# Exponentials in 504-column steps over one ring, a written list of products and expert pieces, and more places for weights and tokens in the tail

## The chip, the cores and the metric

The kernel runs on one core of one Trainium2 chip. The metric is the device time of one execution in microseconds (us), less being better. TensorE is called PE here, its weight loads PEld, VectorE DVE, ScalarE ACT and GpSimd POOL; SP only issues transfers.

## The reference, cut to what matters

```python
# q, k, v: (8, 8, 1152, 64) float32
q_pool = q.reshape(B, H, S // 2, 2, D).mean(axis=3)        # 576 queries a head
scores = (1 / sqrt(D)) * matmul(q_pool, k.transpose(0, 1, 3, 2))
attn = softmax(scores)
x = matmul(attn, v).transpose(0, 2, 1, 3).reshape(8 * 576, 8 * 64)   # 4608 tokens x 512
# mixture of experts: each token has one of 8 experts
for e in range(8):
    mask = domain_id == e
    out[mask] = maximum(x[mask] @ w1[e], 0) @ w2[e]       # 512 -> 1024 -> 512
```

## The kernel before

**Attention.** The 64 heads are taken in 32 pairs. For a pair, PE turns the keys and pooled queries (`turn`, 30 small transposes into one of three score buffers `s`, copied out by DVE into `kq` and `qz`). The scores are computed transposed: nine chunks of 128 keys stand on the partitions, 576 queries along the columns, so a pair has 9 x 576 = 5184 score columns. They are cut into 12 steps of 432 columns (`W`), and a step holds both heads, 864 numbers on each partition. `score(t)` writes a step into a buffer `s` of two PSUM banks (the pool has three of them), and `expo(t)` takes it through one ACT instruction into a buffer `e` of four steps (a ring of four). The maximum isn't subtracted. `av` is one product unit: 5 matmuls of 65 columns that add one chunk of one head, weighted sum and row sum at once, into a bank `acc`; there are 576 units, and after the ninth of a head `evac` divides on DVE into `xb`. When a batch is ready, `put_x` writes it to the token table `x_tok` in DRAM.

**Experts.** Tokens are sorted by expert on DVE during the attention, 5 tiles of 128 tokens for each of 8 experts, 40 tiles. A tile is gathered from `x_tok` (`get_x`, an indirect DMA issued by POOL), turned so that features stand on the partitions, multiplied by `w1` (32 matmuls of 128 columns), clipped at zero, multiplied by `w2` (8 matmuls of 512 columns) and scattered to `out` (POOL). While the attention runs, such tiles are done in pieces: `up` (4 matmuls of 128 columns) and `down` (1 matmul of 512 columns), 16 pieces and one turn a tile.

**What sets the order.** The order in the program is the order in each engine's queue. The main loop goes over `t`, the 384 steps; two steps form a window: score, exponential, the turn where there is one, score, exponential. After them come the product units of a fixed table (`AVS`, three units a window) and then as many pieces as the class `Fill` allows from estimated costs (`C_S`, `C_AV`, `C_P`, a budget `STEP` of 771 ns a step, and `SPAN` for three windows of a pair). 13 tiles are done that way.

**The tail.** After the last exponential come the last 12 units (one bank `acc`, first head to its end, then the second), then the last `put_x`, then the other 27 tiles as runs of tiles of one expert: `stage1` for all tiles of the run, then `stage2` tile by tile. Run 0 is expert 5's first three tiles, whose tokens are already turned in `xf`. The next run's tiles are gathered, and turned by PE (`turn_tile`) between the tiles of `stage2`, or by a transposing DMA on SP (`flip_x`) in the last four runs. Six experts' weights have places; the other two are loaded in the tail into places that come free.

Of the kernel before, what the change touches and what calls it, by code (L numbers as in the profile page):

```python
# [9 lines left out]
P = 128  # L10
# [9 lines left out]
def kernel(  # L20
# [49 lines left out]
    ering = att.enter_context(tc.tile_pool(name="ering", bufs=4))  # L70
# [3 lines left out]
    spsum = att.enter_context(tc.tile_pool(name="spsum", bufs=3, space=bass.MemoryType.PSUM))  # L74
# [7 lines left out]
    qz = [perm.tile([P, Sp], F16, name=f"qz_{i}") for i in range(2)]  # L82
    qps = [perm.tile([P, NJ, 2, D], F16, name=f"qp_{i}") for i in range(2)]
    v16 = [perm.tile([P, NC, 2, DV], F16, name=f"v16_{i}") for i in range(NV)]
# [74 lines left out]
    pre = spsum.tile([P, 2, 512], FP32, name="s")  # L159
# [57 lines left out]
    sc = [perm.tile([P, E, PADC + NT], FP32, name=f"sc{i}") for i in range(2)]  # L217
# [321 lines left out]
    def prep_v(p):  # L539
        nc.vector.tensor_copy(  # L540
            v16[p % NV][:, :, :, 0:D].rearrange("p c h d -> p h c d"), loaded[p]["vs"][:, :, :, :]
        )
# [15 lines left out]
    def turn(p):  # L558
        kp, qp = kpt[p], qpt[p]
        new_kq(p)  # L560
        mt = spsum.tile([P, 2, 512], FP32, name="s")[:, :, :].bitcast(F16)
# [21 lines left out]
    st, et, acc, xb = {}, {}, {}, {}  # L583

    def score(t):
        p, s_ = divmod(t, SPP)
        s = spsum.tile([P, 2, 512], FP32, name="s")
        st[t] = s
        o, u = 0, W * s_
        while o < W:  # L590
            c, q0 = divmod(u + o, Sp)
            n = min(Sp - q0, W - o)
# [7 lines left out]
    def expo(t):  # L600
        p, s_ = divmod(t, SPP)
        if s_ % 4 == 0:
            et[p, s_ // 4] = ering.tile([P, 2, 4 * W], F16, name="e")
        e_ = et[p, s_ // 4]
        o = W * (s_ % 4)
        nc.scalar.activation(  # L606
            e_[:, :, o : o + W], st.pop(t)[:, :, 0:W], AF.Exp, bias=0.0, scale=0.0625
        )

    def av(p, h, c, pool):  # L610
        if c == 0:
            acc[p, h] = pool[0].tile([P, 512], FP32, name=pool[1])
        for i in range(NQ):
            o = (c % 3) * Sp + QO[i]
            nc.tensor.matmul(  # L615
                acc[p, h][:, i * (D + 1) : (i + 1) * (D + 1)],
                lhsT=et[p, c // 3][:, h, o : o + P], rhs=v16[p % NV][:, c, h, 0 : D + 1],
# [20 lines left out]
    ends, cut = (nc.sync, nc.gpsimd), []  # L638

    def put_x(b, i):  # L640
        for lo, hi in zip(CUT, CUT[1:]):
            i_, m = (0, lo) if lo < 64 else (1 + (lo - 64) // P, (lo - 64) % P)
            if i_ == i:
# [7 lines left out]
                cut.append((b, i))  # L651
# [8 lines left out]
    def get_x(pool, e, i):  # L660
        x_ = pool.tile([P, Dm], F16, name="xs")
        mark(x_[0:1, 0:1], True)
        nb = [ib // NQ for k_, ib in zip(KO[1:], IB) if (i + 1) * P <= k_] + [B]
        gather(x_[:, :], grow[:, e * NTC + i : e * NTC + i + 1], nb[0])
# [12 lines left out]
    def load_part(e, j):  # L677
# [6 lines left out]
    AVS = {9 + 2 * g: [(g // 3, c, ACC) for c in range(3 * (g % 3), 3 * (g % 3) + 3)] for g in range(6)}  # L684
    AVS_END = {
        8: [(0, c, ACC) for c in range(4)],
        10: [(0, c, ACC) for c in range(4, 6)],
        12: [(0, c, ACC) for c in range(6, NC)],
        13: [(1, c, ACC) for c in range(NC)],
    }  # L690
    HOLES = ((0, 6), (0, 7), (0, 8), (1, 0))
    STEP, C_MODE, C_S, C_T, C_AV, C_X, C_P, LAG = 771, 190, 183, 440, 147, 220, 217, 250
    SPAN = {2: 1420, 4: 1700, 6: 1260}
# [50 lines left out]
    class Fill:  # L744
        def __init__(self):
            self.blocks, self.cur, self.ready = [], None, 0

        def open(self):
            return self.cur is not None or (self.blocks and self.blocks[0][3])

        def piece(self):
            if self.cur is None:
                self.cur = list(self.blocks.pop(0))
            self.cur[0].pop(0)()
            if not self.cur[0]:
                self.ready = now[0] + self.cur[2]
                self.cur = None

        def able(self, t):
            b = self.blocks[0] if self.blocks else None  # L760
            return b and (b[3] or b[4].get("t", NST) < t < NST - 8 and t >= WSTEP[b[4]["xs"][0]][3] + 14)

        def turns(self, t):
            h0 = tiles[len(turned0)] if len(turned0) < len(tiles) else None
            if h0 and len(turned0) <= len(begun) and got.get(h0["xs"], NST) + 10 <= t < NST - 13:
                return h0
            return None

    fb = Fill()

    turned, turned0, begun, tiles = [], [], [], []
# [13 lines left out]
    def add_tile(e, i):  # L785
        h0 = {"xs": (e, i)}
        tiles.append(h0)
# [33 lines left out]

        for fn, lo, hi in ((up, 0, 4), (up, 4, NF), (down, 0, NF)):
            fb.blocks.append((
                [lambda f=f, fn=fn: fn(f) for f in range(lo, hi)], 222, 1, (fn, lo) != (up, 0), h0
            ))
# [5 lines left out]
    GET = [112, 118, 140, 168, 188, 208, 213, 230, 248, 266]  # L831
    want = [(e, i, at) for (e, i), at in zip(early, GET)]
    want += [(FILL, 0, 296), (0, 2, 304), (FILL, 1, 310), (FILL, 2, 316), (1, 2, 322), (2, 2, 328)]
# [514 lines left out]
```

## Time and profile before

| | |
|---|---|
| median of 3 runs | 430.19 us |
| lowest and highest | 429.98 and 434.39 us |
| the profiled execution, first to last instruction | 436.5 us |
| PE busy, ACT busy, DVE busy | 393.5, 337.4, 229.8 us |
| first exponential starts, last one starts | 7.7 us, 319.5 us |
| first matmul of the tail's run 0 | 323.1 us |

The profiled execution's span is the only time of it that is listed; it is 1.015 of the median of the runs. ACT's work is nearly all exponentials and ends with the attention; PE works from start to end, but its busy time counts a matmul from its start to a modelled end, so that a stretch of matmuls that wait for each other also looks busy. What is read from it are starts, and the gaps that carry a releaser's name.

### The profile page before, as it was taken

What the parts mean: (1) busy time and instruction counts of PE and PEld (TensorE: products, weight loads), DVE (VectorE), ACT (ScalarE), POOL (GpSimd) and SP (SyncE); (2) the same over time, 40 slices, a digit from 0 to 9 for tenths busy, and PEclk for the clock granted to TensorE, in tenths of its full rate; (3) what the DMA queues carried; (4) which work ended last, traced back from release to release, by engine and by line L of the source; (5) the groups of instructions that cost most, each with busy time, mean ns of one, the idle gap of its engine ahead of it and who ended that gap; (6) DMA issues with size and microseconds to landing.
All of it is one profiled execution on the core that took longest, in us unless ns stands there. A gap on an engine that the chain in (4) does not pass through costs nothing. (4 is left out here: it accounts for less than half of the span.)

```text
span 436.5 us, 14439 instructions
## 1 busy us (share of the span) xinstructions
PE 393.5 (90%) x6230; PEld 257.5 (59%) x6230; DVE 229.8 (53%) x628; ACT 337.4 (77%) x445; POOL 185.6 (43%) x304
## 2 busy tenths in 40 slices
PE   7888888888999999999999989989977899999993
PEld 4555555555676766766676666666753565555451
DVE  4588779874565565555656555555331235223221
ACT  5999999999999999999999989999941233323220
POOL 4542233405272742271442436443427586442413
PEclk9699999999999999999999999999998999999999
DMA  8999999994999999798884879975913589998202
GB/s 214 219 234 210 221 233 229 215 221 104 216 230 246 235 222 238 175 230 173 202 191 69 187 132 212 194 179 98 175 52 106 129 158 171 213 172 186 106 25 94
DMA packets 55757, 77.66 MB, mean 178 GB/s; under 512 B 15343, under 2 KB 44432, under 8 KB 55682
## 3 DMA queue, kind: packets, MB, share of 16 engines
q0 software_dynamic: 38384, 66.93, 75.5%
q1 hardware_dynamic: 17026, 9.58, 10.7%
q8 instruction: 50, 0.82, 0.8%
q14 instruction: 25, 0.20, 0.2%
q10 hardware_dynamic: 272, 0.13, 0.1%
HBM read 95.46 MB, written 15.21 MB: 254 GB/s over the span
## 5 line engine op out<-in xcount | busy, mean ns | idle before, releaser
L606 ACT ACTIVATE e<-s 128x864 f16<-128x864 f32 x384 | 306.0, 935 | 7.1 <-PE s L594 4.7
L594 PE MATMUL s<-qz,kq 64*128 64x432 f16 (+2 forms) x1152 | 120.6, 289 | 13.8 <-ACT e L606 10.6
L615 PE MATMUL acc<-v,e 128*128 128x65 f16 x2880 | 121.2, 194 | 9.4 <-DVE xb L630 5.5
L615 PEld LDWEIGHTS <-e 128*128 128x128 f16 x2880 | 104.1, 98 | 38.2 <-DVE xb L630 17.4
L515 POOL DMA_INDIRECT out_dram<-osb,gid x40 | 42.5, 1063 | 80.2 <-DVE osb L816 36.8
L655 POOL DMA_INDIRECT xs<-x_tok,grow x40 | 42.6, 1064 | 74.9 <-DVE xs L93 16.1
L594 PEld LDWEIGHTS <-kq 64*128 64x128 f16 x1152 | 48.2, 94 | 42.8 <-issue 25.1
L114 POOL DMA_DIRECT2D vs<-in_v_dram x32 | 23.7, 741 | 61.0 <-DVE v L540 28.0
L1093 PE MATMUL op<-w2h,hT 128*128 128x512 f16 x208 | 48.3, 387 | 0.0
L1048 PE MATMUL hp<-xt,w1h 128*128 128x256 f16 (+3 forms) x320 | 43.4, 294 | 2.6 <-ACT hT L1053 2.1
L1048 PEld LDWEIGHTS <-w1h 128*128 128x128 f16 x352 | 31.8, 98 | 20.5 <-issue 3.2
L570 DVE COPY kq<-s 128x1152 f16<-128x1152 f16 x31 | 23.5, 758 | 36.1 <-PE s L565 33.7
L1055 DVE TENSOR_SCALAR hT<-hp 128x256 f16<-128x256 f32 (+2 forms) x36 | 20.1, 558 | 40.8 <-PE hp L1048 32.1
L1099 ACT COPY osb<-op 128x512 f32<-128x512 f32 x15 | 8.8, 586 | 42.0 <-PE op L1093 31.1
L1053 ACT ACTIVATE hT<-hp 128x256 f16<-128x256 f32 (+2 forms) x36 | 17.6, 492 | 30.0 <-PE hp L1048 26.8
L628 DVE RECIPROCAL cum<-acc 128x5 f32<-128x5 f32 x48 | 9.2, 192 | 49.6 <-PE acc L615 35.3
L797 PE MATMUL px<-xt,w1h 128*128 128x128 f16 x416 | 33.8, 221 | 0.0
L1093 PEld LDWEIGHTS <-hT 128*128 128x128 f16 x208 | 20.3, 100 | 22.7 <-issue 1.6
L810 PE MATMUL px<-w2h,h 128*128 128x512 f16 x104 | 32.3, 385 | 0.0
L797 PEld LDWEIGHTS <-w1h 128*128 128x128 f16 x416 | 23.4, 98 | 12.3 <-issue 12.1
L531 DVE TENSOR_TENSOR qp<-q 96x768 f16<-96x768 f32 x31 | 29.3, 946 | 1.6 <-DMA q<-in_q_dram 1.6
L123 POOL DMA_DIRECT2D k<-in_k_dram x31 | 23.3, 751 | 4.8 <-DVE vs L93 1.7
(145 smaller groups left out, 325.0 us busy)
## 6 DMA issues: line engine op xcount, KB each, us to landing
q<-in_q_dram POOLq DMA_DIRECT2D x28, 576.0 KB
vs<-in_v_dram POOLq DMA_DIRECT2D x32, 288.0 KB
k<-in_k_dram POOLq DMA_DIRECT2D x31, 288.0 KB
w1h<-in_moe_w_dram POOLq DMA_DIRECT2D x16, 512.0 KB
w2h<-in_moe_w_dram POOLq DMA_DIRECT2D x16, 512.0 KB
x_tok<-xb SPq DMA_DIRECT2D x22, 96.0 KB
q<-in_q_dram SPq DMA_DIRECT2D x3, 576.0 KB
x_tok<-xb SPq DMA_DIRECT2D x22, 64.0 KB
```

The lines of the kernel that those rows point to most:

```text
L114: nc.gpsimd.dma_start(vs[:, :, :, :], v[b, h : h + 2].rearrange("h (p c) d -> p h c d", p=P))
L515: ins = nc.gpsimd.indirect_dma_start(out=dst[:, :], out_offset=bass.IndirectOffsetOnAxis(ap=ap, axis=0), in_=src, in_offset=None, **kw,)
L531: nc.vector.tensor_tensor(out=qp[0:QP, :, :, :].rearrange("p j h d -> p h j d"), in0=q2[:, :, :, 0:D], in1=q2[:, :, :, D : 2 * D], op=ALU.add,
L570: nc.vector.tensor_copy(kq[p][:, :].rearrange("p (c r k) -> p r c k", c=NC, r=2), mt[:, :, 0 : NC * 64].rearrange("p r (c k) -> p r c k", ...
L594: nc.tensor.matmul(s[:, r, o : o + n], lhsT=kq[p][lo:hi, c * P : (c + 1) * P], rhs=qz[p % 2][lo:hi, q0 : q0 + n], start=True, stop=True,)
L606: nc.scalar.activation(e_[:, :, o : o + W], st.pop(t)[:, :, 0:W], AF.Exp, bias=0.0, scale=0.0625)
L615: nc.tensor.matmul(acc[p, h][:, i * (D + 1) : (i + 1) * (D + 1)], lhsT=et[p, c // 3][:, h, o : o + P], rhs=v16[p % NV][:, c, h, 0 : D + 1] ...
L655: nc.gpsimd.indirect_dma_start(out=dst, out_offset=None, in_=x_dram[0 : 1 + nb * Sp, :], in_offset=bass.IndirectOffsetOnAxis(ap=ap, axis=0),)
L797: nc.tensor.matmul(m[:, f % 4, :], lhsT=wts[e][0][:, cc, f * P : (f + 1) * P], rhs=h0["xt"][:, cc, :], start=cc == 0, stop=cc == ND - 1,)
L810: nc.tensor.matmul(h0["o"][:, :], lhsT=h0["h"][:, f, :], rhs=wts[e][1][:, f, :], start=f == 0, stop=f == NF - 1,)
L1048: nc.tensor.matmul(hp_[:, lo : lo + n], lhsT=w1h[:, cc, f * P : (f + 1) * P], rhs=xt[:, cc, lo : lo + n], start=cc == 0, stop=cc == ND - 1,)
L1093: nc.tensor.matmul(op_[:, :], lhsT=hT[:, f, i * P : (i + 1) * P], rhs=w2h[:, f, :], start=f == 0, stop=f == NF - 1,)
```

## The change

- A step has 504 columns (`CW`) instead of 432: 330 exponentials, the last of 72 columns, which run on over the borders of chunks and pairs. They are written to one tile `er` of 14 chunks, used as a ring. The three score buffers are named tiles taken in turn (`next_s`).
- `AVS`, `Fill` and their costs are gone. `PLAN` has a word for each of 165 windows: `A3` is three product units, `P4` four pieces or turns of a tile, `K2` two matmuls on zeros; what stands ahead of a `/` goes between the window's two scores, the rest behind. The list holds 238 pieces and turns (14 tiles of 17), 564 units and 36 zeros. The gathers' times (`GET`, `want`) are rewritten.
- The last 12 units take a bank for each head, in an order in which chunk 8 comes last for both.
- In the tail the gathers for the first run that has none are issued right behind the last `put_x`. A run of one tile, (expert 4, tile 2), stands behind run 0. In run 0 the next run's turns wait until ahead of its last tile. Transposing DMAs serve the last two runs. A seventh weights place (`wnext`) holds expert 6's weights, loaded during the first two runs; `tx` has 4 buffers, `ob` 7, `xsb` 13. The row-sum check is done in two parts. Some small tiles move to other memory.

```diff
-    spsum = att.enter_context(tc.tile_pool(name="spsum", bufs=3, space=bass.MemoryType.PSUM))
+    spsum = att.enter_context(tc.tile_pool(name="spsum", bufs=1, space=bass.MemoryType.PSUM))
...
+    RING, CW = 14, 504
+    er = pair.tile([P, 2, RING * Sp], F16, name="er")
...
+    sbuf = [spsum.tile([P, 2, 512], FP32, name=f"s{i}") for i in range(3)]
...
+    def next_s():
+        used[0] += 1
+        return sbuf[(used[0] - 1) % 3]
...
+    COL = list(range(0, NPAIR * NC * Sp, CW)) + [NPAIR * NC * Sp]
...
+    def expo(k):
+        o, w = COL[k] % (RING * Sp), COL[k + 1] - COL[k]
         nc.scalar.activation(
-            e_[:, :, o : o + W], st.pop(t)[:, :, 0:W], AF.Exp, bias=0.0, scale=0.0625
+            er[:, :, o : o + w], st.pop(k)[:, :, 0:w], AF.Exp, bias=0.0, scale=0.0625
         )
...
-    AVS = {9 + 2 * g: [(g // 3, c, ACC) for c in range(3 * (g % 3), 3 * (g % 3) + 3)] for g in range(6)}
...
-    STEP, C_MODE, C_S, C_T, C_AV, C_X, C_P, LAG = 771, 190, 183, 440, 147, 220, 217, 250
-    SPAN = {2: 1420, 4: 1700, 6: 1260}
+    LAST = (spsum, "s")
+    PLAN = (
+        "- K3/K3 K3/K2 A2K2 A5 K2/A K2/A K2/A7 "
...
+        "A/A4 A3 A6 A3 K2/AK2 A/A4 PA3 P4A2 "
+        "A2P4 A5P3 PA3 A6 P4A2 PA5 P4A2 A4 "
...
+        "AP4 A2P4 A7P2 A6 P6 "
+    ).split()
...
+    def window(k, t):
...
+        inner, _, line = PLAN[k // 2].rpartition("/")
...
+        score(k)
+        expo(k)
+        if k in TURN:
+            turn(TURN[k])
+        steps(t, k, inner)
+        score(k + 1)
+        expo(k + 1)
+        steps(t, k, line)
...
+        if t == NST:
+            left = [u[1:] for u in units]
+            lead = [u for u in left if u < (0, 7)] + [u for u in left if (1, 0) <= u < (1, 7)]
+            for h, c in lead + [(0, 7), (1, 7), (0, 8), (1, 8)]:
+                product(t, (NPAIR - 1, h, c), LAST if h else ACC)
...
             plan_runs()
+            e, i0, i1 = next(r for r in runs if (r[0], r[1]) not in xs)
+            for i in range(i0, i1):
+                get_x(fxs, e, i)
...
+            if left[e] == NA - 1 and (e, NA - 1) in xs and len(runs) == 1:
+                runs.append((e, NA - 1, NA))
...
-    tx = ctx.enter_context(tc.tile_pool(name="tx", bufs=3, reuse_waits="tile"))
+    tx = ctx.enter_context(tc.tile_pool(name="tx", bufs=4, reuse_waits="tile"))
...
+    wlast.append(ctx.enter_context(tc.tile_pool(name="wnext", bufs=1, reuse_waits="tile")))
...
-    FLIP = len(runs) - 4
-    rest, wq = list(range(HELD, E)), []
+    FLIP = len(runs) - 2
+    wq, wts[HELD] = load_w(HELD, wlast[1])
...
-            k_ == len(runs) - 1,
+            k_ == len(runs) - 1, first=n - 1 if k_ == 0 else 0,
```

PE around a turn, before (the rows of `s` are scores, `ident,kp` and `ident,qp` the turn, `acc` product units, `px` expert pieces; weight loads and repeats left out):

```order
L594 MATMUL s<-qz_97,kq 128x432
...
L565 MATMUL s<-ident_103,kp 128x64
...
L565 MATMUL s<-ident_103,qp_98 128x64
...
L594 MATMUL s<-qz_97,kq 128x144
...
L594 MATMUL s<-qz_97,kq 128x288
...
L810 MATMUL px<-w2h,h_3469 128x512
...
L615 MATMUL acc<-v_0_100,e 128x65
```

The same place in the changed program:

```order
L613 MATMUL s_121<-qz_97,kq 128x72
...
L579 MATMUL s_119<-ident_104,kp 128x64
...
L579 MATMUL s_119<-ident_104,qp_98 128x64
...
L633 MATMUL acc<-v_0_100,er 128x65
...
L613 MATMUL s_120<-qz_97,kq 128x504
...
L633 MATMUL acc<-v_0_100,er 128x65
```

One product unit moved in between the turn and the window's second score; four units and no piece follow that score, where three units and a piece did.

PE from run 0's end on, before (`hp<-xf` is run 0's `stage1`, `hp<-ident,xs` a turn of gathered tokens, `op` is `stage2`, `hp<-xt` the next run's `stage1`):

```order
L1048 MATMUL hp<-xf,w1h 128x384
...
L1066 MATMUL hp<-ident_103,xs 128x128
...
L1093 MATMUL op<-w2h,hT 128x512
...
L1066 MATMUL hp<-ident_103,xs 128x128
...
L1093 MATMUL op<-w2h,hT 128x512
...
L1048 MATMUL hp<-xt,w1h 128x256
```

The same place in the changed program:

```order
L1072 MATMUL hp<-xf,w1h 128x384
...
L1117 MATMUL op<-w2h,hT 128x512
...
L1090 MATMUL hp<-ident_104,xs 128x128
...
L1117 MATMUL op<-w2h,hT 128x512
...
L1072 MATMUL hp<-xt,w1h 128x128
...
L1090 MATMUL hp<-ident_104,xs 128x128
...
L1117 MATMUL op<-w2h,hT 128x512
...
L1072 MATMUL hp<-xt,w1h 128x256
```

Two of run 0's three tiles of `stage2` moved ahead of the first turn, and that turn is of (4, 2), gathered during the attention; the first tokens gathered behind the last `put_x` are turned behind the one-tile run's `stage1`.

## Rows read from the trace of the kernel before

**Rows 1.** The page: its span and its costliest group.

```profile
span 436.5 us, 14439 instructions
...
L606 ACT ACTIVATE e<-s 128x864 f16<-128x864 f32 x384 | 306.0, 935 | 7.1 <-PE s L594 4.7
```

**Rows 2.** Exponentials (L606) by stretch: us, ACT busy (count), PE clock granted, DMA share, GB/s.

```profile
7.60:18.10 10.50, 9.74 (x13) 0.67 1.08 215
18.10:102.90 84.80, 84.75 (x108) 1.00 1.09 215
102.90:200.50 97.60, 95.82 (x122) 1.00 1.06 220
200.50:320.50 120.00, 115.73 (x145) 1.00 0.76 156
```

**Rows 3.** ACT timeline, start us, us: nine unbroken; the last two of these; the attention's last two.

```profile
19.64 7.16 ACT L606 ACTIVATE e<-s 128x864 f16<-128x864 f32 x9
...
25.03 1.77 ACT L606 ACTIVATE e<-s 128x864 f16<-128x864 f32 x2
...
318.71 1.67 ACT L606 ACTIVATE e<-s 128x864 f16<-128x864 f32 x2
```

**Rows 4.** ACT groups by form, the other activations: busy us, mean ns of one.

```profile
L1053 ACT ACTIVATE hT<-hp 128x256 f16<-128x256 f32 x16 | 6.1, 386 | 7.5 <-PE hp L1048 6.2 <-issue 1.4
L1053 ACT ACTIVATE hT<-hp 128x384 f16<-128x384 f32 x12 | 5.9, 492 | 12.6 <-PE hp L1048 10.8 <-DVE tot L1121 0.9 <-issue 0.8
L1053 ACT ACTIVATE hT<-hp 128x640 f16<-128x640 f32 x8 | 5.6, 704 | 9.8 <-PE hp L1048 9.8
```

**Rows 5.** PE timeline: an ordinary window, then a window with a turn.

```profile
198.22 0.54 PE L594 MATMUL s<-qz,kq 64*128 64x288 f16 x6
198.70 0.82 PE L810 MATMUL px<-w2h,h 128*128 128x512 f16 x3
...
199.90 0.36 PE L594 MATMUL s<-qz,kq 64*128 64x432 f16 x2
...
203.02 0.36 PE L594 MATMUL s<-qz,kq 64*128 64x432 f16 x2
...
203.84 0.36 PE L594 MATMUL s<-qz,kq 64*128 64x144 f16 x4
...
204.91 0.86 PE L594 MATMUL s<-qz,kq 64*128 64x288 f16 x6
```

**Rows 6.** PE and POOL timeline from the last units to run 1.

```profile
321.55 1.54 PE L615 MATMUL acc<-v,e 128*128 128x65 f16 x45 [0.81 <-DVE xb L630]
...
324.13 2.67 POOL L645 DMA_DIRECT2D x_tok<-xb  x5 [13.18 <-DVE xs L93]
...
329.44 1.01 POOL L655 DMA_INDIRECT xs<-x_tok,grow  x1 [1.23 <-PE hp L1048]
...
332.29 0.61 PE L1066 MATMUL hp<-ident,xs 128*128 128x128 f16 x4 [3.00 <-DMA xs<-x_tok,grow]
...
342.93 2.34 PE L1048 MATMUL hp<-xt,w1h 128*128 128x256 f16 x20 [2.06 <-ACT hT L1053]
```

**Rows 7.** Windows of the tail: us, busy of PE, PEld, DVE, ACT, POOL, granted clock, DMA, GB/s.

```profile
328.70:332.30 3.60, 0.60 (x5) 0.15 (x3) 0.56 (x1) 0.47 (x1) 2.41 (x5) 0.95 0.33 112
332.30:336.00 3.70, 3.70 (x17) 1.81 (x18) 0.00 (x0) 0.66 (x2) 3.04 (x7) 0.59 0.38 103
```

**Rows 8.** The chain that ended last: start us, us, what.

```profile
355.80 0.22 PE hp L1066 x4
...
357.75 3.52 PE hp L1048 x32
...
394.32 8.69 PE hp L1048 x64
403.02 8.63 PE op L1093 x40
...
430.36 0.42 POOL out_dram L515
```

More of the change, by code (lines that the diff above doesn't have):

```diff
@@ L216 @@
     ief = perm.tile([P, E], FP32, name="ief")
-    sc = [perm.tile([P, E, PADC + NT], FP32, name=f"sc{i}") for i in range(2)]
+    SCW = 2 * E * (PADC + NT)
+    sc = [
+        xf[:, i * SCW : (i + 1) * SCW].bitcast(FP32).rearrange("p (e i) -> p e i", e=E)
+        for i in range(2)
+    ]
     oh = perm.tile([P, E, NT], F16, name="oh")
@@ L560, in turn @@
         new_kq(p)
-        mt = spsum.tile([P, 2, 512], FP32, name="s")[:, :, :].bitcast(F16)
+        mt = next_s()[:, :, :].bitcast(F16)
         for c in range(NC + NJ):
@@ L582, with when, score @@
     rrs = cum[:, :, :].rearrange("p e i -> p (e i)")
[L583 to L592, printed above, removed]
+    st, acc, xb = {}, {}, {}
+    COL = list(range(0, NPAIR * NC * Sp, CW)) + [NPAIR * NC * Sp]
+    NK = len(COL) - 1
+    def when(k):
+        return -(-COL[k] // W)
+    def score(k):
+        s = next_s()
+        st[k] = s
+        o, w = 0, COL[k + 1] - COL[k]
+        while o < w:
+            p, u = divmod(COL[k] + o, NC * Sp)
+            c, q0 = divmod(u, Sp)
+            n = min(Sp - q0, w - o)
             for r, (lo, hi) in enumerate(HALF):
@@ L742 @@
     now = [0]
[L744 to L771, printed above, removed]
+    turned, begun, blocks, cur = [], [], [], []
     def spare(shape, dt=FP32):
@@ L786, in add_tile, with flip @@
         h0 = {"xs": (e, i)}
-        tiles.append(h0)
+        def flip():
+            h0["xt"] = fill.tile([P, ND, P], F16, name="xt0")
+            turn_x(h0["xt"][:, :, :], e, i)
         def up(f):
@@ L885 @@
         main = t < NST
+        if t in heads:
+            window(heads[t], t)
         if main and s_ == 0 and 0 < p and p + 3 < NPAIR:
@@ L936 @@
-        if t == NST - 2 and not fb.open() and len(turned0) < len(tiles):
-            x_ = tiles[len(turned0)]
-            if got.get(x_["xs"], NST) + 10 <= t:
-                x_["xt"] = fill.tile([P, ND, P], F16, name="xt0")
-                turn_x(x_["xt"][:, :, :], *x_["xs"])
-                turned0.append(x_["xs"])
-                x_["t"] = t
+        if t == NST:
[3 more added lines that the diff above has]
+                product(t, (NPAIR - 1, h, c), LAST if h else ACC)
@@ L952 @@
                 want.pop(0)
-        if first and t >= got.get(first[0], NST) + 8:
+        if first and t >= max(got.get(first[0], NST) + 8, FLIPS[first[0][1]]):
             e, i = first.pop(0)
@@ L1072, in turn_tile, with stage2 @@
             nc.scalar.copy(dst, pv)
-    def stage2(w2h, hT, n, ids, between=(), split=False):
+    def stage2(w2h, hT, n, ids, between=(), split=False, first=0):
         between = list(between)
         for i in range(n):
-            for _ in range(-(-len(between) // (n - i))):
+            for _ in range(-(-len(between) // (n - i)) if i >= first else 0):
                 between.pop(0)()
@@ L1272, in again @@
                     )
-        ah.close()
     def one_tile(w, og, oi):
```

231 lines of the change are left out of this document (110 added, 121 removed), and 17 rows, old and new, of the table PLAN.

## The prediction

> **What bounds the kernel now.** I read the page first, then the exponentials by stretch, then ACT's and PE's timelines where the exponentials slow down, and last the tail. The page shows ACT with 306.0 us of exponentials and only 7.1 us of idle ahead of them [rows 1]: from 7.6 to 320.5 us the exponentials set the time. But "busy" counts each from its start to its end, and they overlap. What counts is the pitch, start to start: two starts seven exponentials apart are 19.64 and 25.03 [rows 3], so 0.770 us. 384 of them would take 295.7 us; from 7.6 to 320.4 (318.71 + 1.67) [rows 3] are 312.8. So some 17 us are exponentials that start late. By stretch (length over count less one, since both ends of a stretch count) the pitch is 0.875, 0.793, 0.807 and 0.833 [rows 2]: against 0.770 that loses 1.3, 2.4, 4.5 and 9.1 us. The loss is largest where expert pieces fill PE, so there PE is the partner that comes late.
>
> Rows 5 show how. An ordinary window with three pieces and three product units goes from 198.22 to 199.90, 1.68 us, and two pitches are 1.54: PE loses 0.14. The window with a turn goes from 203.02 to 204.91, 1.89 us. The turn takes one of the three score buffers, so that the second score (203.84) waits until an exponential has freed one; behind it stand a piece and three units, and the next window's scores begin only at 204.91, 1.07 us later. Their exponential is due two pitches after that freeing, 1.54, and the two score groups need about 0.3 each: nothing is left.
>
> From 323.1 us PE is alone. In the steady part it needs 8.69 + 8.63 = 17.32 us for five tiles, 3.46 each [rows 8]. But from run 0's start (321.55 + 1.54 = 323.09) [rows 6] to run 3's (357.75) [rows 8] it does seven tiles in 34.7 us, where 7 x 3.46 and six turns of 0.22 [rows 8] make 25.5. [...]
>
> **The change, part by part.** Sums are against the profiled span of 436.5 us; at the end I scale by 430.19 / 436.5 = 0.9855 to the median of the runs.
>
> 1. *Longer exponentials.* The other activations cost (704 - 386) / 384 = 0.828 ns for each number on a partition, and the middle form lies on that line [rows 4]. A step goes from 864 to 1008 numbers: 0.770 + 144 x 0.000828 = 0.889 us. 329 of them and a short last one make about 292.7 us against 295.7: gain 3.0. If the pitch had no fixed part it would be 0.898 and the gain nothing; I take 3.0, since both differences of rows 4 give the same slope. The scores need as many matmuls and columns as before.
>
> [...]
>
> 2. *The list in place of the budget.* A window now has 2 x 0.889 = 1.778 us. From the row of 1.68 I take off three pieces of 0.216 (8.63 / 40) [rows 8] and three units of 0.171 (1.54 / 9) [rows 6]: 0.52 for two scores and the switches of shape, and 0.06 more for 144 more columns. From the first piece on the list has 111 windows with 238 pieces (2.14 each, 0.46 us), 387 units (3.49, 0.60) and 20 turns (0.64 each [rows 5], 0.12 a window): 0.52 + 0.06 + 0.46 + 0.60 + 0.12 = 1.76. That is tight, 99% (some of the turn's 0.64 is waiting, so it is less in truth), and before it was no better: 221 pieces and turns over the 131 windows from step 122 on, the earliest at which `Fill` may turn a tile, make about 1.5 of 1.54. So the fourteenth tile is paid from the longer windows, and what decides is the order. A turn window now has one unit ahead of its second score, where PE waited anyway, and at most four units or a piece and three units behind it: about 0.7 us, and with two scores of 0.3 there are 1.3 of 1.78. After a window of 2.1 us the list puts lighter ones, and units that open a new head stand behind pieces, so that DVE's evacuation is covered. The lateness that is left I estimate at 5 us, below the 7 us that 330 exponentials would lose at the rate of the stretch without pieces (0.793 - 0.770); its ends are 1 and the old 17. Gain 17 - 5 = 12. The 36 matmuls on zeros lie in windows with no piece; they cost nothing while the window's sum stays under 1.78, and if not, about 0.12 each.
>
> 3. *The last units.* PE waited 0.81 us for DVE between the heads [rows 6], and run 0 began 2.7 us after the last exponential's end. With a bank for each head that wait goes; 12 units and six pieces still stand behind the last score. I take 1.5 us: gain 1.2, between 0 and 2.
>
> 4. *Fourteen tiles instead of thirteen in the attention*: one tile less in the tail, 3.5 us.
>
> 5. *The way into the tail.* The first gather was issued at 329.44, 6.4 us after the last unit, and its tokens were turned from 332.29 on, 9.2 us after it [rows 6]. That stays: the last `put_x` (POOL's five until 326.80) [rows 6] and the landing are the same. But PE now has run 0 and the first half of a one-tile run ahead of it, 3 x 3.46 + 1.7 = 12.1 us: the gather is hidden with 2.9 us to spare, and with the gap goes the low clock. I take 6.2 of the 9.2 us as gained and 3 as staying (the wait on ACT has no cause that I can name). Four more tiles are turned by PE instead of SP: -0.9. Expert 6's weights are issued on POOL between gathers for later runs, four issues that delay those gathers; they are needed 7 us later at the earliest, so I price that at 0. If the cover is gone, the 3.0 us and the clock are back. Gain 5.3, between 0 and 8.
>
> 6. *DMA.* Up to 102.9 us the DMA share is 1.09 [rows 2]: full. The loads come as many columns ahead as before, while a column takes 0.889 / 1008 instead of 0.793 / 864, 4% less. If the loads can't follow, 4% of 84.8 us is lost, 3.4; I take 0, since no exponential there waits for longer than in an undisturbed stretch by more than 0.02 us on average.
>
> Sum: 3.0 + 12 + 1.2 + 3.5 + 5.3 = 25.0, so a span of 411.5 us, times 0.9855: **405.5 us**.
>
> **The rivals.**
> - *PE becomes the bound.* 1.76 of 1.78 leaves no room; if a unit, a turn or a switch costs more in the new order, the exponentials stay as late as they were. Then term 2 is gone: 423.5, or 417.4 us. For it speaks the sum, against it that the lateness of before sits at the turns, which are lightened.
> - *The tail's gap stays*, because the weights' transfers or DRAM writes delay the first gathers beyond 12.1 us, or another buffer is waited for: term 5's 6.2 us are lost, 417.7, or 411.6 us.
> - *Everything fits*: lateness of 1 us and 1 us lost in the tail: 405.5, or 399.6 us.
> - *Slower: the exponentials no longer overlap.* From the seventeenth on each now carries a wait on its own engine, where before one in four did. If that wait is for the exponential just before, each starts when that has ended: one takes 0.935 [rows 1] where the pitch is 0.770, so 0.165 more each, 329 x (0.889 + 0.165) = 346.8 us for the attention instead of 312.8. With terms 3 to 5 the span is 436.5 + 34.0 - 10.0 = 460.5, or 453.8 us. It decides as soon as the wait reaches back less than two exponentials. Against it: the first sixteen have no such wait, and 16 x 504 is the ring's length, so it should be for the one that wrote the same columns a round before.
>
> **How the numbers follow.** Forecast 0.62 (its own range 401 to 411: lateness 2 to 9 us, terms 3, 5 and 6 at their nearer ends); PE the bound 0.16; the tail's gap 0.14; everything fits 0.05; slower 0.03. For 8 in 10 the range reaches from 400 over the tail's gap to PE as the bound, 418. A measurement of this kernel tells about 1% from no change, so faster means below 425.9: all cases but the last, and a little for what I have not seen: 0.95, 0.02, 0.03.
>
> **What would show it.** Term 1: the pitch of undisturbed exponentials at 0.89 us. Term 2: from first to last exponential some 298 us, and no stretch over 0.91 a step. Term 3: run 0 within 2 us of the last exponential's end. Term 4: 448 `up` matmuls. Term 5: no wait of PE for a gather, and a granted clock of 1.00 from the last unit on; run 0 to the end of the last `stage2` in about 97 us. I would be wrong if the pitch is above 0.90, if exponentials wait for scores in each turn window as before, or if the tail has a new gap of over 3 us.

## The result and the profile after

The changed kernel takes **416.18 us** (median of 4 runs, 415.09 to 417.49), the kernel before 432.29 beside it (4 runs, 429.98 to 437.72): ratio 0.9697, interval 0.9654 to 0.974. The forecast was 405.5, its range 400 to 418. The direction came as forecast, and so did the shorter time of the exponentials and the covered gap in the tail; the gain is about 14 us (430.19 less 416.18) instead of 25. To read what follows: times have two levels, the kernel before taking 427 to 434 us in most executions of four jobs and 436 to 442 in two others, the changed one 415 to 418 in two of the four and 432 to 444 in the one of the two that ran it.

The page after: the span, the engines, the exponentials, and a part to which the page before has no counterpart, how long transfers took to land.

```profile
span 414.4 us, 14867 instructions
...
PE 386.7 (93%) x6350; PEld 260.6 (63%) x6350; DVE 232.0 (56%) x638; ACT 331.1 (80%) x396; POOL 182.9 (44%) x303
...
L621 ACT ACTIVATE er<-s 128x1008 f16<-128x1008 f32 x330 | 299.2, 1096 | 3.7 <-PE s L613 3.1
...
q<-in_q_dram POOLq DMA_DIRECT2D x28, 576.0 KB, 9.5
```

The exponentials by stretch, after, as [rows 2] of before (us, ACT busy and count, PE's granted clock, DMA share, GB/s):

```profile
7.30:52.00 44.70, 42.22 (x46) 0.96 1.13 221
52.00:109.00 57.00, 56.23 (x63) 1.00 1.00 205
109.00:200.00 91.00, 90.88 (x102) 1.00 1.10 228
200.00:310.10 110.10, 109.85 (x123) 1.00 0.82 169
```

And two starts from ACT's timeline, 21 exponentials apart in an unbroken row:

```profile
42.20 3.71 ACT L621 ACTIVATE er<-s 128x1008 f16<-128x1008 f32 x4
...
60.91 3.98 ACT L621 ACTIVATE er<-s 128x1008 f16<-128x1008 f32 x4
```

The pitch is 18.71 / 21 = 0.891 us (0.8905 in finer figures; [rows 3] gave 0.770 before). With length less (count less one) times the pitch, as in the prediction, the four stretches lose 4.6, 1.8, 1.1 and 1.5 us, 9.0 in all (9.3 from each start to the next): where expert pieces fill PE, from 109 us on, the exponentials are now hardly late, and half of what is lost lies ahead of 52 us.

PE's timeline where the attention ends:

```profile
311.36 0.31 PE L633 MATMUL s<-v,er 128*128 128x65 f16 x5
311.53 5.51 PE L1072 MATMUL hp<-xf,w1h 128*128 128x384 f16 x32
...
322.27 0.83 PE L1072 MATMUL hp<-xt,w1h 128*128 128x128 f16 x12
323.29 1.37 PE L1072 MATMUL hp<-xt,w1h 128*128 128x128 f16 x20 [0.18 <-ACT hT L1077]
324.50 0.69 PE L1090 MATMUL hp<-ident,xs 128*128 128x128 f16 x8
...
344.32 1.91 PE L1072 MATMUL hp<-xt,w1h 128*128 128x256 f16 x16 [1.31 <-ACT hT L1077]
...
405.19 1.98 PE L1108 MATMUL op<-w2h,hT 128*128 128x256 f16 x16
```

Run 0 starts 1.5 us after the last exponential's end (310.04), the first gathered tokens are turned at 324.50 with no wait in front ([rows 6] had 3.00), and from run 0 to the last matmul's end it is 95.6 us. PE waits only at 323.29 and 344.32.

### The profile page after: what moved, and what is told of

It reads as the page before. It is cut to its first block, busy times and chain, and to the rows that moved or that the text cites. A ratio compares the mean times of both kernels' runs of the same rounds, so it can differ in the third digit from the quotient of the medians.

```text
span 414.4 us, 14867 instructions
## 1 busy us (share of the span) xinstructions
PE 386.7 (93%) x6350; PEld 260.6 (63%) x6350; DVE 232.0 (56%) x638; ACT 331.1 (80%) x396; POOL 182.9 (44%) x303
## 4 chain that ended last, share of the span: by engine, by line
PE 68%; ACT 10%; DMA 8%; DVE 6%; issue 4%; POOL 1%; SPq 1%; POOLq 0%; ACTq 0%; DVEq 0%
PE s L613 17%; PE acc L633 17%; ACT er L621 9%; PE hp L1072 9%; PE op L1117 8%; PE px L821 6%; PE px L808 6%; DMA k<-in_k_dram 4%; DMA out_dram<-osb,gid 3%; PE s L579 3%; DVE kq L584 1%; DMA x_tok<-xb 1%; SPq L664 1%; DVE xb L648 1%; DVE qz L589 1%
## 5 line engine op out<-in xcount | busy, mean ns | idle before, releaser
L621 ACT ACTIVATE er<-s 128x1008 f16<-128x1008 f32 x330 | 299.2, 1096 | 3.7 <-PE s L613 3.1
L633 PE MATMUL acc<-v,er 128*128 128x65 f16 x2835 | 118.3, 194 | 7.3 <-DVE xb L648 3.8
L633 PEld LDWEIGHTS <-er 128*128 128x128 f16 x2880 | 101.0, 98 | 36.7 <-issue 17.6
L613 PE MATMUL s<-qz,kq 64*128 64x504 f16 (+6 forms) x1152 | 113.6, 287 | 7.1 <-ACT er L621 4.2
L613 PEld LDWEIGHTS <-kq 64*128 64x128 f16 x1152 | 44.7, 94 | 39.6 <-issue 22.3
L1072 PEld LDWEIGHTS <-w1h 128*128 128x128 f16 x384 | 33.7, 98 | 15.6 <-issue 1.8
L1072 PE MATMUL hp<-xt,w1h 128*128 128x256 f16 (+2 forms) x352 | 42.0, 277 | 1.5 <-ACT hT L1077 1.5
L1079 DVE TENSOR_SCALAR hT<-hp 128x256 f16<-128x256 f32 (+3 forms) x40 | 20.1, 504 | 37.0 <-PE hp L1072 29.1
L1077 ACT ACTIVATE hT<-hp 128x256 f16<-128x256 f32 (+3 forms) x40 | 17.7, 449 | 23.9 <-PE hp L1072 23.9
L808 PEld LDWEIGHTS <-w1h 128*128 128x128 f16 x448 | 25.3, 98 | 4.9 <-issue 4.7
L813 DVE TENSOR_SCALAR h<-px 128x512 f16<-128x512 f32 x28 | 19.3, 690 | 15.3 <-PE px L808 15.3
```

Of the source, the lines that this page charges most:

```text
L613: nc.tensor.matmul(s[:, r, o : o + n], lhsT=kq[p][lo:hi, c * P : (c + 1) * P], rhs=qz[p % 2][lo:hi, q0 : q0 + n], start=True, stop=True,)
L621: nc.scalar.activation(er[:, :, o : o + w], st.pop(k)[:, :, 0:w], AF.Exp, bias=0.0, scale=0.0625)
L633: nc.tensor.matmul(acc[p, h][:, i * (D + 1) : (i + 1) * (D + 1)], lhsT=er[:, h, o : o + P], rhs=v16[p % NV][:, c, h, 0 : D + 1], start=c = ...
L808: nc.tensor.matmul(m[:, f % 4, :], lhsT=wts[e][0][:, cc, f * P : (f + 1) * P], rhs=h0["xt"][:, cc, :], start=cc == 0, stop=cc == ND - 1,)
L1072: nc.tensor.matmul(hp_[:, lo : lo + n], lhsT=w1h[:, cc, f * P : (f + 1) * P], rhs=xt[:, cc, lo : lo + n], start=cc == 0, stop=cc == ND - 1,)
```

## The same kernels on other chips

First came the unedited kernel before, twice, to see what one measurement is worth.

> The kernel before, unchanged, for a second profile. My theory of the missed size: the profiled execution that I read (span 436.5 us) held some 8 us of delays that an ordinary execution of the same kernel does not have, so that an ordinary one has a time of about 430 us, a span of about 428, and the delays are found in single places (the wait for the gathered tokens and the slow clock behind it, the 2.1 us wait in run 1, the late exponential at 261 us). Rival: the profile stretches everything, so that span and time differ by about 1.5% here too and each part is shorter by that share. Ratio to the kernel before: 1.00.

> The same again, for a third profile. By my theory the attention (first to last exponential) is the same within 1 us in the three profiles and the difference sits in the tail or in single waits; by the rival all parts differ in the same proportion.

They took 438.41 us (10 runs; ratio 0.9992, 0.9954 to 1.003) and 436.77 (one run). With them ran two edits of the changed kernel. The loads of the weights of experts 1 to 4 left out (their tiles are computed with expert 0's):

```diff
+        if 0 < e < FILL:
+            wts[e] = wts[0]
+            return
```

> The changed kernel without the loads of the weights of experts 1 to 4 during the attention (their tiles are computed with expert 0's weights), so that 16 MB fewer are read up to step 192. Theory A: the 5.6 us of late exponentials before 109 us come from full DMA engines (term 6, which I priced at 0), then the pitch of the stretch from 20 to 109 us falls from 0.924 to about 0.90 and the kernel gains 2 to 3 us in that stretch, ratio to the kernel before about 0.963 where the changed kernel has 0.970. Theory B: they come from the order on DVE, whose evacuations stand behind sorting work and prep copies; then the stretch stays at 0.92 and the time changes by under 1 us.

And the 36 matmuls on zeros left out (every `K2` and `K3` of the list):

```diff
-        "- K3/K3 K3/K2 A2K2 A5 K2/A K2/A K2/A7 "
+        "- - - A2 A5 /A /A /A7 "
```

> The changed kernel without its 36 matmuls on zeros. If they hold PE's clock up in the first 20 us (granted clock 0.87 there, 0.67 in the kernel before), the clock falls to about 0.7 in that stretch and the first exponentials lose 0.5 to 1.5 us. If they are only extra work among late scores, the clock stays within 0.05 and the stretch gets shorter by up to 1 us.

They took 435.28 (ratio 0.9878, 0.9841 to 0.9916) and 436.54 (0.9919, 0.988 to 0.9959): neither loses nor gains a few us against 416, both are 20 us slower. Either the edits mattered far beyond their size, or the chip did. Their traces still answer what they were made for. Without the loads the DMA share from 52 to 109 us is 0.72 instead of 1.00, and 63 exponentials lie there in both, so full DMA engines cost nothing in that stretch. Without the matmuls on zeros the granted clock from 7.5 to 20.5 us is 0.87, as it is in the profile after, so nothing shows that they hold it up. The next job had the unedited changed kernel and three edits of it.

> The changed kernel, unedited, beside its variants. Two theories for the 20 us that the two edited kernels of the first job took beyond the changed kernel's 416. Theory A (the chip): its edges don't matter, it was a chip on which transfers and PE's signals come later; then the unedited kernel takes 432 to 437 here too, with first-to-last exponential of 311 to 314 us and 105 us from run 0 on. Theory B (the edits): loads and zeros matter in themselves; then it takes 415 to 418 here, 0.95 to 0.96 of the kernel before.

```diff
-        "AP4 A2P4 A7P2 A6 P6 "
+        "A A2 A7 A6 - "
```

(the end of the list; the 17 P's of its last windows are gone)

> The changed list without its last 17 pieces and the turn that belongs to them, so that 13 tiles are done in the attention, as before, and 27 in the tail. By term 4 of the prediction it is 3.5 us slower than the unedited changed kernel (one tile of 3.46 us more in the tail, nothing back in the attention, where PE kept up). Rival: PE is the bound in the last windows, and 16 pieces of 0.22 us and a turn less give the 3.5 us back before the tail: no difference, and less lateness in the last 60 us of exponentials.

```diff
-        ... A/A3 ... A/A4 ... A/PA2 ...
+        ... A1A3 ... A1A4 ... A1PA2 ...
```

> The changed list with the units that stand between the two scores of a turn window moved behind the second score; same work, other order. If the written order earns its gain at the turns (term 2), each of some 16 such windows gets back a wait of about 0.2 to 0.5 us: 3 to 7 us slower than the unedited changed kernel, and lateness higher by as much. Rival: the three score buffers given out in rotation and the lighter windows behind a turn absorb it: within 1 us.

```diff
-            if left[e] == NA - 1 and (e, NA - 1) in xs and len(runs) == 1:
-                runs.append((e, NA - 1, NA))
-                left[e] = NA
...
-    FLIP = len(runs) - 2
+    FLIP = len(runs) - 4
...
-        for kn in (k_ + 1, k_ + 2, k_ + 3):
+        for kn in (k_ + 1, k_ + 2):
```

> The changed kernel with the old way into the tail: no one-tile run between run 0 and run 1, tokens turned two runs ahead instead of three, three tx places, SP's transposing loads from the fourth run from the end on; the seventh weights place stays. By term 5: PE waits some 3 us for the first gather again, then runs at the lower clock for some us, and the time from run 0 to the end grows by 4 to 6 us. Rival: the wait on ACT and others are the larger part of the 9.2 us and stay as they are: within 1.5 us.

The unedited kernel took 439.31 (431.79 to 444.26), ratio 0.9922 (0.9859 to 0.9985): theory A, though the time is above the 432 to 437 that it gave. The edits, 439.5 (1.0044, 1.0009 to 1.0079), 438.02 (0.9979, 0.9939 to 1.0018) and 437.96 (0.9986, 0.9954 to 1.0019), could not be told from it by their medians. In this job a gain of 14 us shrinks to some 3 or to nothing, and no edit above is the reason. Each of these later jobs ran on a chip of its own, so the runs do not tell a chip from a job.

Where do 20 us go? In e5 the exponentials are late by 21.2 us, in e9 below by 9.6, and from run 0 on it takes 104.2 us instead of 94.2. Between a profiled execution at 437 us and one at 416 of the same program PE falls behind in small jumps. One of them, PE and then DVE around the turn of a pair, in e5:

```profile
165.59 0.43 PE L579 MATMUL s<-ident,kp 64*128 64x64 f16 x18
165.85 0.34 PE L579 MATMUL s<-ident,qp 64*128 64x64 f16 x12
...
167.07 0.76 DVE L584 COPY kq<-s 128x1152 f16<-128x1152 f16 x1 [1.80 <-PE px L787]
...
168.31 0.39 PE L613 MATMUL s<-qz,kq 64*128 64x216 f16 x4 [0.69 <-DVE qz L589]
```

and the same place in the unedited kernel on a third chip (the run e9 below):

```profile
164.28 0.43 PE L579 MATMUL s<-ident,kp 64*128 64x64 f16 x18
164.54 0.34 PE L579 MATMUL s<-ident,qp 64*128 64x64 f16 x12
...
165.06 0.76 DVE L584 COPY kq<-s 128x1152 f16<-128x1152 f16 x1 [1.09 <-PE s L579]
...
165.93 0.76 PE L613 MATMUL s<-qz,kq 64*128 64x144 f16 x8
```

The turn's matmuls take the same time. But DVE, idle and waiting for their completion (the profile names the signal that came last), starts 0.88 us after their end in the first (165.85 + 0.34 = 166.19, 167.07) and 0.18 in the second (164.88, 165.06). The times at which PE's completion semaphore changes show the same: in the first, three changes come at 166.98, 167.04 and 167.10, as if released together. Such bursts (two or more changes 0.04 to 0.08 us apart), counted over a trace, are 15 to 25 in each of the eight profiled executions above, and 2 in the profile after. How much of the 20 us they make was not counted. The trace from which the prediction was made has **23**. It has another mark that is on the page: no row of its part on transfers gives a time to land, and the same holds for the pages of those eight.

## The changed kernel and its parts where signals come in time

> The changed kernel unedited, as the base of this job. If what takes 20 us more than on the first chip is a matter of the chip or of the execution, it is 415 to 418 or 436 to 441 here, nothing between, and in the second case PE's completion signals again come in bursts of two or three 0.06 us apart (about 19 places; the profiled execution of 414.4 has two), those of three at 138, 167, 215 and 244 us.

416.18 us again (414.94 to 416.69) against 429.38 of before, ratio 0.9687 (0.9616 to 0.9758), span 414.1, two bursts; nothing between the two levels. Its page, like that of e12, gives landing times only in the rows of SP's transfers, so that a few missing times are no mark of bursts; every other profiled execution from here on has them in all rows of its page. In the same job, on the same chip: a tile's turn moved one window on where it stands behind a pair's turn,

```diff
-        PA2 P4 ... PA3 AP4 ... PA3 A2P2 ... PA3 A6
+        A2 P5 ... A3 AP5 ... A3 A2P3 ... A3 A6P
```

> The changed list with the piece that turns an expert tile (four transposes) moved one window on in the four windows where it stands right behind a pair's turn (list entries 69, 84, 110 and 125). Theory T: PE's signals are held where the tile's transposes follow the turn's thirty; then the four bursts of three are gone and with them four waits of 0.7 to 1.2 us: 3 to 5 us faster than the unedited kernel where that one takes 436 to 441, and the same where it takes 416. Rival: what holds the signals is not these instructions; the bursts move with them or appear in other windows, and the time stays within 1.5 us.

the pair's turn by 15 transposes instead of 30,

```diff
-            for r, (lo, hi) in enumerate(HALF):
-                nc.tensor.transpose(
-                    mt[:, r, c * 64 : c * 64 + 64],
...
+            n = P if c < NC else QP
...
+            nc.tensor.transpose(
+                mt[:, c // 8, c % 8 * P : c % 8 * P + n],
...
```

> The turn of a pair by 15 transposes of 128 rows instead of 30 of 64 (two at a time), and one copy less on DVE. PE needs some 0.4 us more for each of 31 turns. Theory D: so many short instructions within 0.5 us hold PE's signals; with half as many in twice the time the holds at the turns go, and it is 2 to 8 us faster where the unedited kernel takes 436 to 441. Rival: PE has 1.76 of 1.78 us in a window, by term 2's sum, and 0.4 us more in each turn window makes the exponentials later: 2 to 6 us slower on any chip.

and the tile's turn by products with the identity.

```diff
-        m = spare([P, ND, P], F16)
+        m = spare([P, ND, P])
...
-            nc.tensor.transpose(
-                m[:, cc, :], in_=xs[e, i][:, cc * P : (cc + 1) * P], identity=ident16[:, :]
+            nc.tensor.matmul(
+                m[:, cc, :], lhsT=xs[e, i][:, cc * P : (cc + 1) * P], rhs=ident16[:, :],
+                start=True, stop=True,
```

> A tile is turned in the attention by four products with the identity into 32-bit PSUM instead of four transposes into 16-bit PSUM; DVE's copy then takes about 0.69 us instead of 0.41. If writing 16-bit PSUM behind the turn's 16-bit writes is what holds PE's signals, the bursts of three at the four windows go: 3 to 5 us faster where the unedited kernel takes 436 to 441. Rival: no difference in the holds, and 14 copies of 0.28 us more on an engine with room: within 1 us.

There were no bursts to take away here, so what T and D say of them stays untried. As changes of order they tell something else. Four pieces moved by one window cost 2.8 us (419.02, ratio 0.9778, 0.97 to 0.9856): the third and fourth stretches now lose 3.7 and 3.8 us, where the profile after has 1.1 and 1.5.

```profile
109.00:200.00 91.00, 88.73 (x99) 1.00 1.06 224
200.00:313.30 113.30, 111.57 (x124) 1.00 0.80 166
```

(91 less 98 pitches, 113.3 less 123). The longer turns cost 4.6 us (420.81, 0.9817, 0.9731 to 0.9903). A turn takes 0.93 us there instead of 0.60 (medians of the traces of e11 and e9), so 31 of them add some 10 us of PE time, of which about half shows. The products with the identity make no difference (415.94).

The next job asked for the kernel before in an undisturbed trace, and for terms 4 and 5, with the edits of e8 and e6 again.

> The kernel before, unedited, for a profiled execution on a chip where it takes 427 to 430. If the trace from which the prediction was made came from an execution in which PE's signals were held (bursts of signals at 23 places), then here the bursts are few, the span is 425 to 428, and what is 8 to 10 us less than 436.5 lies in the lateness of the exponentials (16.6 us there) and in the time from run 0 on (106.0 there). Rival: the lateness of before is that of its order, 15 us or more here too, and the 8 us lie elsewhere.

> The old way into the tail in the changed kernel (as in the earlier run of it: no one-tile run, tokens turned two runs ahead, three tx places, SP's transposing loads from the fourth run from the end on), on a chip where the unedited changed kernel takes 416. By term 5 PE waits some 3 us for the first gather again and runs at the lower clock behind it: 4 to 6 us slower, all of it from run 0 on. Rival: a later gather is hidden all the same, within 1.5 us.

> 13 tiles in the attention instead of 14, 27 in the tail, on a chip where the unedited changed kernel takes 416. Term 4: one tile of 3.46 us more in the tail, and since the last exponentials are hardly late (1.8 us over the last 58,000 columns) nothing to give back in the attention: 3 to 3.5 us slower. Rival: leaving 17 pieces out takes the lateness of the last stretch away: 1.5 to 2 us slower.

```diff
-    WSTEP = [[20 + 40 * e + 10 * j for j in range(4)] for e in range(4)]
+    WSTEP = [[28 + 40 * e + 10 * j for j in range(4)] for e in range(4)]
...
-        if t in (12, 16):
-            (prep_k if t == 12 else prep_q)(2)
+        if t in (15, 17):
+            (prep_k if t == 15 else prep_q)(2)
```

> The changed kernel with two things later: DVE's casts of the third pair's k and q (steps 15 and 17 instead of 12 and 16), which wait there for their loads with the evacuations of the products queued behind them, and the weights of the first four experts (each 8 steps later). Theory: of the 9.6 us by which exponentials are late, 5 to 6 us are lost before 60 us in DVE's wait of 4 us for the third pair's k and behind it; 2 to 4 us faster than the unedited changed kernel. Rival: the loads are late because the transfers are full (DMA share 1.2 from 16 to 28 us), and whoever waits, the turn waits: within 1 us.

The unedited kernel before took 437.4 in the profiled execution and 428.52 in the other (432.96), with no burst at all: most of its excess is a pause of 5.6 us (below). The unedited changed kernel was not run in this job or the next, so that the differences from 416.18 below go across jobs; the traces carry the readings. 13 tiles took 419.39 (0.9722, 0.9666 to 0.9779), 3.2 us more than the 416.18 of 14; by the ratios it is 1.1 to 1.5 us more, and the intervals overlap, so the times alone do not decide between term 4 and its rival. The traces do: from run 0 to the last matmul's end it is 97.7 us (312.92 to 410.67) instead of 94.2, and the last stretch loses as much as in e9; only 0.7 us come back, where run 0 follows the last exponential sooner. The rows of e9 on which this and the table below rest, ACT's last exponentials, run 0's start and the last matmuls:

```profile
304.99 5.87 ACT L621 ACTIVATE er<-s 128x1008 f16<-128x1008 f32 x7
...
312.29 0.97 PE L1072 MATMUL hp<-xf,w1h 128*128 128x384 f16 x5
...
404.49 1.98 PE L1108 MATMUL op<-w2h,hT 128*128 128x256 f16 x16
```

The old way into the tail took 423.82 (420.02, 420.77, 426.87 and 428.86; before 430.76 beside it), so 4 us more than 416.18 at least. Its span is 418.8 against 414.1, and PE's timeline has the gap of term 5 back:

```profile
311.89 5.48 PE L1068 MATMUL hp<-xf,w1h 128*128 128x384 f16 x32
...
322.87 0.40 PE L1086 MATMUL hp<-ident,xs 128*128 128x128 f16 x4 [2.04 <-DMA xs<-x_tok,grow]
324.50 0.40 PE L1086 MATMUL hp<-ident,xs 128*128 128x128 f16 x4 [1.24 <-DMA xs<-x_tok,grow]
324.74 2.72 PE L1113 MATMUL op<-w2h,hT 128*128 128x512 f16 x7
...
377.65 2.56 PE L1068 MATMUL hp<-xt,w1h 128*128 128x128 f16 x20 [1.73 <-DMA xt<-xs]
...
409.71 1.98 PE L1104 MATMUL op<-w2h,hT 128*128 128x256 f16 x16
```

with a lower granted clock behind it (0.61 from 324.5 to 327.9 us, where the profile after has 1.00 from 311.5 to 330.0; 7 matmuls take 2.72 us, where [rows 8] have 8.63 for 40). From run 0 on it takes 99.8 us, 5.6 more than 94.2. The easier start took 415.71 (0.9661, 0.9592 to 0.973). The first stretch in e9, the first in e10, whose list is the same up to there, and the first and third in e16:

```profile
7.80:52.00 44.20, 41.03 (x45) 0.96 1.13 226
```

```profile
7.50:52.00 44.50, 43.03 (x48) 1.00 1.14 232
```

```profile
7.80:52.00 44.20, 43.62 (x48) 1.00 1.13 226
...
109.00:200.00 91.00, 89.73 (x100) 1.00 1.09 231
```

The first loses 2.4 us (44.2 less 47 pitches) instead of 5.0 (less 44), but the third 2.8 instead of 1.1. And e10, without this edit, loses only 2.6 in the first. The half us that is left is less than these runs can tell.

> The kernel before once more, for a profiled execution at 427 to 430. In the last one (437.4) PE started nothing for 5.6 us at 289 us and its tail took 100.6 us from run 0 on, with PE's signals never held. Theory: without that pause the span is about 426, the lateness of the exponentials 12 to 15 us and the tail again 100 to 101 us; then the changed kernel's 9.6 us and 94.2 us leave 3 to 5 us for term 2 and 6.4 for terms 4 and 5 together. Rival: lateness of 16 us and more belongs to the kernel before on any chip.

> The changed list with the units that stand between the two scores of a turn window moved behind the second score, as in the earlier run of it, on a chip where the unedited changed kernel takes 416. If the written order is what takes the wait out of the turn windows (term 2), 15 windows lose about 0.2 us each again, more lateness by 2 to 4 us and as much time. Rival: the rotation of the three score buffers and the lighter windows behind take it up: within 1 us.

The kernel before took 431.46 in the profiled execution, 438.36 in the other; the units moved behind the second score (the edit of e7 again) 416.93 (0.9681, 0.9604 to 0.9758), the rival: what stands between the scores of a turn window earns nothing that can be measured. It could not earn much: by the list only 12 of the 31 turn windows have a unit there, and 6 of the 20 from the first piece on; the edit also moves units in three windows next to a turn. The run e17 is the undisturbed trace of before that was missing: no bursts, landing times on its page. Its exponentials by stretch, and PE and ACT at the attention's end:

```profile
7.90:52.00 44.10, 43.38 (x56) 0.92 1.14 228
52.00:109.00 57.00, 56.77 (x73) 1.00 0.99 203
109.00:200.00 91.00, 90.29 (x115) 1.00 1.08 225
200.00:317.30 117.30, 114.40 (x144) 1.00 0.84 159
```

```profile
314.49 2.75 ACT L606 ACTIVATE e<-s 128x864 f16<-128x864 f32 x3
...
319.97 3.50 PE L1048 MATMUL hp<-xf,w1h 128*128 128x384 f16 x20
...
329.15 0.48 PE L1066 MATMUL hp<-ident,xs 128*128 128x128 f16 x4 [3.00 <-DMA xs<-x_tok,grow]
...
336.48 3.66 PE L1048 MATMUL hp<-xt,w1h 128*128 128x256 f16 x32
...
351.26 0.93 PE L1048 MATMUL hp<-xt,w1h 128*128 128x256 f16 x7
...
419.99 2.03 PE L1084 MATMUL op<-w2h,hT 128*128 128x256 f16 x16
```

With the pitch of the trace behind the prediction, 0.7708 in finer figures, its stretches lose 1.7, 1.5, 3.1 and 7.1 us (13.2 from start to start), and its tail takes 422.02 - 319.97 = 102.1 us. The trace behind the prediction had 16.6 and 106.0.

## Why the forecast was 10 us too low

Term by term, the undisturbed trace of before (429.4) against that of after in the run e9 (414.1); both from their timelines:

| | forecast gain | before | after | gain |
|---|---|---|---|---|
| 1, exponentials at their pitch | 3.0 | 384 x 0.7708 = 296.0 | 329 x 0.8905 + 0.1 = 293.1 | 2.9 |
| 2 and 6, lateness | 12, and 0 | 13.2 | 9.6 | 3.6 |
| 3, last exponential to run 0 | 1.2 | 2.7 | 1.4 | 1.3 |
| 4, one tile less in the tail | 3.5 | | | 3.5 (e15) |
| 5, the rest of the tail | 5.3 | 102.1 | 94.2 | 7.9 - 3.5 = 4.4 |
| sum | 25.0 | | | 15.7 (spans: 15.3) |

Of the 13.2 us of lateness 1.8 are a pause of PE in that execution (last section). The medians of the two kernels in the job of e9 are 13.2 us apart as well, 2.1 less than the two spans; that fits if most executions lack such a pause, which is not shown.

Of the signs that the prediction named, the pitch, run 0 within 2 us, the 448 `up` matmuls (the page after has x448) and a tail without a wait for a gather came; a stretch at most 0.91 a step did not, the first two have 0.99 (44.70 / 45) and 0.92 (57.00 / 62).

**Terms 1, 3 and 4 came as worked out.** The pitch is 0.8905 where 0.889 was forecast, so the slope of [rows 4] held beyond its longest form. Term 4 measured 3.5 in the tail, with 0.7 given back ahead of it.

**The scaling failed, and this is most of it.** The prediction set its sum against a profiled span of 436.5 and then took 0.9855 of the result "to the median of the runs". An execution's listed time is its span and 2.0 us (416.44 and 414.4; 437.4 and 435.3): so the profiled one was a run of some 438.5 us, not a long recording of one of 430. What it had more than those lay where the change was to gain: 3.4 us of lateness (16.6 against 13.2) and 3.9 in the tail (106.0 against 102.1). The sum counted these as gains, and the factor took them off once more. Without it the forecast is 411.5 + 2.0 = 413.5, 2.7 below the result: of the 10.7 us that are missing 6.0 are the factor and 2.0 the step from span to listed time, which it left out. One part can be named: the wait of 2.06 us on ACT in [rows 6], for which the prediction had no cause, is not in e17, where the same 32 matmuls run unbroken (336.48), and in the trace behind the prediction four changes of PE's semaphore come between 341.99 and 342.16, ahead of that wait's end at 342.93. The three runs shown gave 429.98 to 434.39, so a trace of 436.5 was a warning, and it went unheeded.

**Term 2 was mis-sized, and term 6 with it.** Lateness was to fall from 17 to 5; in undisturbed traces it falls from 13.2 to 9.6. After 109 us the list does what was forecast: 10.2 us (8.4 without the pause) become 2.6. Ahead of 52 us it goes the other way, from 1.7 to 4.6 and, in e9, 5.0. That is the step "I take 0" of term 6: its bound was 3.4, and 2.9 to 3.3 came (2.0 to 2.5 if counted from start to start). The waits before 52 us (us in total, times, longest) in e9 and, behind it, in e17:

```profile
DVE kp L560 <- DMA k<-in_k_dram: 5.2, 2, 4.1
```

```profile
DVE kp L546 <- DMA k<-in_k_dram: 1.3, 1, 1.3
```

The run e16, in which DVE comes to that cast later (it waits 0.6 us), loses 2.6 us less, but that the wait is the cause is not shown. Six undisturbed profiled executions share the list up to 52 us, and they lose between 2.3 and 5.6 us there from start to start: 2.3 in e10, where the longest wait is 2.5 us and the granted clock stays at 1.00; 3.7 to 4.2 in the profile after, e9, e12 and e14; 5.6 in e15, with a wait of 4.6 us and a granted clock of 0.50 from 24 to 28 us. So the loss goes with the wait, with the clock behind it, and with chance from one execution to the next; no run separates them, and why e16's gain does not reach the end is open. The reason given for the list, lighter turn windows, is not borne out: "A turn window now has one unit ahead of its second score" holds for 6 of the 20 turn windows with pieces, most others have a piece and two or three units behind it as before, and e18 shows that those units are not what gains. That the placing of the pieces matters is shown by e10, at 0.7 us for each of four; which of its features gains is open.

**Term 5 was right in kind and nearly in size**: 4.4 instead of 5.3 (2.9 against the 100.6 us that e13's tail takes), and e14 shows 5.6 lost when its parts are undone (its transposing DMAs for the last four runs add a wait of 1.73 us of their own). The 9.2 us of which the prediction takes 6.2 are 34.7 less 25.5: the rows show 3.00 of waiting for the first tokens and 2.06 on ACT [rows 6], and 3.7 us at a granted clock of 0.59 behind the first wait [rows 7]; no run shows the 6.2 as such.

**The rivals.** That the tail's gap stays, or that the exponentials no longer overlap, did not happen. PE as the bound holds in a weaker form: some 10 us more of PE work in e11 cost 4.6.

## What to carry to other kernels

Before a sum is set against a trace, compare the trace's own time with the runs: if it is longer than most of them, ask where the excess lies, and do not scale it away, least of all when it may lie in the places that the change is to relieve. A page without a landing time in any row comes here from an execution whose signals come late (15 to 25 bursts in each of the nine such traces). A written order of instructions is worth what its worst windows leave: four pieces in the wrong window cost 2.8 us here, and its gain of 14 us in one job was 3 or none in another.

## What the runs showed of the hardware

**PE's completion signals came late, in bursts**: 0.8 us at the turn shown above (166.98 against a modelled end of 166.19; 0.09 in e9). The six disturbed executions of the changed kernel and its edits all have a burst near that place (165.3 to 168.3 us), while the matmuls and the transfers take no longer (a packet of 1152 bytes 0.107 us in the median, in e5 and in e9). Executions with 15 or more bursts have fewer records of semaphore changes: 12% in e5 (5835 against 6624 in e9), 10% in the trace behind the prediction (6125 against 6798 in e17). Both marks come together here, and no run here separates the recording from the chip; the cause stays open. Theories T and D are open with it: e10 to e12, made for them, met a chip without bursts.

**PE may have run out of instructions**, as two pauses are read here. In e13 and e17 PE stops behind the same matmul, in the middle of a product unit, with no semaphore to wait for. PE's timeline in the one and in the other:

```profile
283.01 0.40 PE L615 MATMUL acc<-v,e 128*128 128x65 f16 x8
289.02 0.57 PE L615 MATMUL acc<-v,e 128*128 128x65 f16 x7 [5.61 <-issue]
```

```profile
282.85 0.39 PE L615 MATMUL acc<-v,e 128*128 128x65 f16 x7 [1.80 <-issue]
```

In e13 the transfers between 272.6 and 286.0 us have no packet of the instruction queue q8, where one comes every 4 to 11 us otherwise during the attention; the next lies between 286.0 and 289.1, in whose view of the transfers it stands:

```profile
DMA packets 311, 0.66 MB, mean 212 GB/s; under 512 B 40, under 2 KB 233, under 8 KB 310
...
q8 instruction: 1, 0.02, 3.0%
```

Its packet took from 286.1 to 287.6, and PE went on at 289.0, 1.4 us later; in e17 the packet ended at 281.35 and PE went on at 282.85, 1.5 us later. In a trace without a pause there (the one behind the prediction) the packet ended at 279.2, and the same matmul started at 284.4. So a late block of instructions fits both pauses; that this queue brings PE's instructions is read from its name and from these times. The profile gives both waits no name but "issue" on PE, and in e13 the granted clock behind it was 0.61 from 289 to 296 us.
